# Converting double weights to float32 on chip: the exponent's offset moved from VectorE into ScalarE's scale

## The chip, the core and the metric

The kernel runs on one core of one Trainium2 chip. The metric is the device time of one execution in microseconds (us), lower is better. One core has a matrix engine (PE, TensorE), a vector engine (DVE, VectorE), a scalar engine (ACT, ScalarE), a general engine (POOL, GpSimd) and a sync engine (SP, SyncE) that issues most DMAs. Each engine works through its own instructions in order and waits on semaphores for the others.

## The reference

```python
x = attention(q, k, v, beta)          # a delta-rule recurrence over 768 steps, 32 heads of 48
x = x.transpose(...).reshape(3072, 384)
h = np.maximum(x @ w_in, 0.0)          # 384 x 2048
x = (h * h @ w_out).astype(np.float32)  # 2048 x 384
g = x @ w_gate                          # 384 x 1536
silu = g * (1.0 / (1.0 + np.exp(-g)))
return (silu * (x @ w_val) @ w_out2).astype(np.float32)
```

The five weight matrices arrive as float64, everything else as float32.

## The kernel before

There are three parts: the attention recurrence over six blocks J of 128 steps, a first pair of matrix products (w_in, relu squared, w_out), called moe1, and a second (w_gate, w_val, silu, w_out2), called moe2. For precision every operand of a large product is split into a high part rounded to PE's fp32r format and the rest, and three products are summed: high by high, high by rest, rest by high. PE's stream is written in program order; it computes moe1 of block J while the attention of block J + 1 is prepared, and moe2 at the end.

The weights come as 64-bit words, two int32 each, and are turned into float32 on chip, in pieces of 128x768 numbers. One `Piece` works as follows (line numbers of the kernel before):

- L171: ACT takes the absolute value of the upper word, read as a float, into the buffer `f` (there is one such buffer).
- L178: DVE takes the maximum of `f` and a constant. L180: DVE shifts `f` left by 3 bits and clears the top bits. L184: DVE puts in sign and the exponent's top bit from the upper word. L189: DVE adds the top three bits of the lower word. These are the piece's `STEPS`, four.
- `high` (L202): ACT copies the result into the weight tile, rounded. `low` (L205): the difference, on DVE in most of block 0, on POOL for the weights of moe2.

The 16 pieces of w_in and w_out (the last cut in two halves) are converted in the first 190 us, beside the end of the first attention block and moe1 of block 0; odd pieces are w_in, even ones w_out. `conv` is called with a number of pieces or half pieces while the attention starts up, and counts `int(STEPS * n)` steps; what is converted by then is `PRE`. From then on `conv_to` keeps the conversion a fixed number of steps ahead of the units of moe1. `conv_one` makes one step; it begins the next piece (its L171) behind the third operation, and behind the last operation it sends out the `low` of the piece before and this piece's `high`. The 18 pieces of moe2 are converted late in moe1, from 664 to 762 us, one `conv2_step` at a time.

A unit of moe1 is the following: PE makes h (L794, with x's high `xh` and rest `xl`), ACT relu (L797), square rounded to `hh` (L798) and square again (L802), DVE the rest `hl` (L804), then PE the second product `ps_y` (L820), whose last three groups read `hl`. In block 0 a unit is made for half the tokens (256 columns); later units have 512. The order of DVE, ACT and POOL in the overlapped parts is set by a scheduler at build time, with DVE, ACT and POOL in program order only in the startup and DVE later; so an edit of the pieces moves neighbours.

In moe2, ACT copies x rounded (`x2h`, L872), DVE makes the rest (`x2l`, L873).

Of the kernel before, what the change touches and what calls it, by code (L numbers as in the profile page):

```python
# [11 lines left out]
ACTF = mybir.ActivationFunctionType  # L12
ALU = mybir.AluOpType
AX = mybir.AxisListType


TINY = 2.0 ** -15


@with_exitstack  # L20
def delta_attention_moe_moe2_kernel(
# [35 lines left out]
    nc = tc.nc  # L57
# [12 lines left out]
    is64 = w_in.dtype == mybir.dt.int64  # L70
# [82 lines left out]
    class Piece:  # L153
# [2 lines left out]

        STEPS = 4 if is64 else 1

        def __init__(self, raw, place, blocks, lo):
            self.d = raw.rearrange("p (b f z) -> p z b f", b=blocks, z=Z)
            self.place, self.blocks, self.lo_eng = place, blocks, lo
            self.v = self.d[:, 1 if is64 else 0].bitcast(F32)
            self.left = self.STEPS
            if is64:

                n = self.d.shape[2] * self.d.shape[3]
                f = rp.tile([128, PIECE], F32, tag="f", bufs=1, name="f")[:, 0:n]
                self.f = f.rearrange("p (b f) -> p b f", b=blocks)  # L170
                nc.scalar.activation(out=self.f, in_=self.v, func=ACTF.Abs)  # L171
            self.steps = self.run()

        def run(self):
            if is64:
                f, fi = self.f, self.f.bitcast(I32)

                nc.vector.tensor_scalar(out=f, in0=f, scalar1=TINY, scalar2=None, op0=ALU.max)  # L178
                yield
                nc.vector.tensor_scalar(  # L180
                    out=fi, in0=fi, scalar1=3, scalar2=0x3FFFFFFF, op0=ALU.logical_shift_left, op1=ALU.bitwise_and
                )
                yield
                nc.vector.scalar_tensor_tensor(  # L184
                    out=self.d[:, 1], in0=self.d[:, 1], scalar=-0x40000000, in1=fi,
                    op0=ALU.bitwise_and, op1=ALU.bitwise_or,
                )
                yield
                nc.vector.scalar_tensor_tensor(  # L189
                    out=self.d[:, 1], in0=self.d[:, 0], scalar=29, in1=self.d[:, 1],  # L190
                    op0=ALU.logical_shift_right, op1=ALU.bitwise_or,
                )
            yield
# [23 lines left out]
    conv1 = [(pc, kd, 0) for pc in range(NP1) for kd in range(2)] + [(*LAST, 1)]  # L217
# [3 lines left out]
    making = []  # L221
    STEPS = Piece.STEPS

# [13 lines left out]
    def flush():  # L237
        while pending:
            pending.pop().low()
# [3 lines left out]
    def begin(job, lo):  # L243
        pc, kd, e = job
        if job in begun or job not in loaded:
            return
        raw = loaded.pop(job)

        def place():
            if e == 0:  # L250
                w1[pc, kd] = wp.tile([128, 2 * PIECE], F32R, tag="w", name="w1")
            return w1[pc, kd][:, e * PIECE:(e + 1) * PIECE] if job[:2] == LAST else w1[pc, kd]

        begun[job] = Piece(raw, place, 1 if job[:2] == LAST else 2 if kd else 2 * KD, lo)

    def conv_one(lo):

        if not making:
            job = conv1.pop(0)
            begin(job, lo)  # L260
            making.append(begun.pop(job))
        making[0].step()
        if making[0].left == STEPS - 3 and conv1:
            begin(conv1[0], lo)
        if making[0].left == 0:
            flush()
            making[0].high()
            pending.append(making.pop())

    def converted():  # L270

        return STEPS * (NCONV - len(conv1)) - sum(m.left for m in making)

    def conv_to(steps, lo):

        while converted() < min(steps, STEPS * NCONV) and (making or conv1[0] in loaded or conv1[0] in begun):
            conv_one(lo)

    def need(m, kd):

        i = 2 * (m // 2) + kd + (1 if (m // 2, kd) == LAST and m % 2 else 0)
        conv_to(STEPS * (i + 1), nc.vector)
        if converted() < STEPS * (i + 2):
# [640 lines left out]
    def run_all(names):  # L924
        for n in names:
            run(n)
# [31 lines left out]
    for b0 in (0, 64):  # L958
        nc.gpsimd.affine_select(
            out=mask[b0:b0 + 64], in_=mask[b0:b0 + 64], compare_op=ALU.is_ge, fill=1.0,  # L960
            base=0, pattern=[[-1, 64]], channel_multiplier=1,
        )
    for c in P2:
        k_load(1, c, nc.gpsimd)
    q_load(0, nc.gpsimd)
    run(("sq", 0, 0))
    run_all(("gram0", 0, 0, p) for p in P2)
    run(("root", 0, 0))
    run(("mb0", 0, 0, 0, nc.vector))
    run(("mb0", 0, 0, 1, nc.gpsimd))  # L970
# [238 lines left out]
```

## Time and profile before

| | |
|---|---|
| time, median of 3 runs | 1181.83 us (1181.17 to 1186.19) |
| profiled execution | 1185.92 us, its span 1184.1 us |
| mean granted TensorE clock | 0.946 of full speed |
| busy in the span: PE, DVE, ACT, POOL | 1087.6, 645.5, 385.2, 271.3 us |

Busy time is the time in which an engine executed instructions, so an engine that is 55% busy over the whole span can still be fully taken in a stretch of it. PE's time is 92% of the span; the question is what PE waits for in the other 8%, and where.

### The profile page before, as it was taken

What the parts mean: (1) busy time and instruction counts of PE and PEld (TensorE: products, weight loads), DVE (VectorE), ACT (ScalarE), POOL (GpSimd) and SP (SyncE); (2) the same over time, 40 slices, a digit from 0 to 9 for tenths busy, and PEclk for the clock granted to TensorE, in tenths of its full rate; (3) what the DMA queues carried; (4) which work ended last, traced back from release to release, by engine and by line L of the source; (5) the groups of instructions that cost most, each with busy time, mean ns of one, the idle gap of its engine ahead of it and who ended that gap; (6) DMA issues with size and microseconds to landing.
All of it is one profiled execution on the core that took longest, in us unless ns stands there. A gap on an engine that the chain in (4) does not pass through costs nothing. (4 is left out here: it accounts for less than half of the span.)

```text
span 1184.1 us, 25132 instructions
## 1 busy us (share of the span) xinstructions
PE 1087.6 (92%) x10863; PEld 905.3 (76%) x10863; DVE 645.5 (55%) x1116; ACT 385.2 (33%) x711; POOL 271.3 (23%) x394
## 2 busy tenths in 40 slices
PE   4378778999999999999999987899999999999998
PEld 4367667777888888788888865688888888888887
DVE  3859995456547546555543699834334343343333
ACT  1034563332233233323333666422122122122222
POOL 5067100480183166128000233300000000000000
PEclk8557887999999999999999999999999999999999
DMA  8537440461434326132211445301001010010000
GB/s 237 132 81 280 93 104 20 95 160 43 91 66 115 77 49 168 46 69 59 77 29 27 161 143 177 107 1 54 1 1 54 1 54 1 1 54 1 27 1 27
DMA packets 129119, 88.23 MB, mean 75 GB/s; under 512 B 103216, under 2 KB 107952, under 8 KB 129008
## 3 DMA queue, kind: packets, MB, share of 16 engines
q1 hardware_dynamic: 126656, 76.79, 24.6%
q0 software_dynamic: 2208, 9.57, 2.5%
q8 instruction: 85, 1.39, 0.5%
q10 hardware_dynamic: 144, 0.26, 0.1%
q14 instruction: 26, 0.21, 0.1%
HBM read 63.54 MB, written 23.07 MB: 73 GB/s over the span
## 5 line engine op out<-in xcount | busy, mean ns | idle before, releaser
L794 PE MATMUL ps_h<-xh,w 128*128 128x512 f32 (+1 forms) x684 | 215.3, 377 | 6.1 <-DVE w L205 5.5
L820 PE MATMUL ps_y<-hh,w 128*128 128x512 f32 (+1 forms) x654 | 158.5, 378 | 1.8 <-DVE w L205 1.7
L794 PEld LDWEIGHTS ps_h<-xh,w 128*128 128x128 f32 x684 | 129.9, 199 | 28.4 <-DVE w L205 6.1
L887 PE MATMUL ps_g<-x2h,w 128*128 128x512 f32 x432 | 145.9, 392 | 0.5 <-ACT x2h L872 0.5
L887 PE MATMUL ps_v<-x2h,w 128*128 128x512 f32 x432 | 144.9, 389 | 0.0
L797 ACT ACTIVATE r<-ps_h 128x512 f32<-128x512 f32 (+1 forms) x114 | 60.2, 528 | 248.0 <-PE ps_h L794 232.7
L891 DVE SCALAR_TENSOR_TENSOR th<-th,ps_g 128x512 f32<-128x512 f32 x72 | 49.4, 686 | 167.1 <-ACT th L890 166.9
L820 PEld LDWEIGHTS ps_y<-hh,w 128*128 128x128 f32 x654 | 113.4, 194 | 22.1 <-DVE w L205 2.2
L794 PE MATMUL ps_h<-xl,w 128*128 128x512 f32 (+1 forms) x342 | 126.7, 371 | 2.3 <-POOL xl L675 1.7
L800 DVE TENSOR_TENSOR r<-r 128x512 f32<-128x512 f32 (+1 forms) x72 | 50.3, 699 | 133.1 <-ACT hh L798 132.9
L912 PE MATMUL ps_o<-ph,w 128*128 128x512 f32 x432 | 111.9, 389 | 2.5 <-ACT ye L836 2.5
L820 PE MATMUL ps_y<-hl,w 128*128 128x512 f32 (+1 forms) x327 | 87.7, 378 | 18.9 <-DVE hl L804 18.9
L453 POOL TENSOR_TENSOR TMP<-T 128x30 f32<-128x30 f32 (+9 forms) x150 | 84.4, 563 | 82.5 <-DMA T<-m_scr 46.6
L890 ACT ACTIVATE th<-ps_g 128x512 f32<-128x512 f32 x72 | 43.0, 597 | 175.8 <-PE ps_g L887 175.8
L804 DVE TENSOR_TENSOR hl<-r,hh 128x512 fp32r<-128x512 f32 (+1 forms) x114 | 76.5, 671 | 43.0 <-ACT r L802 37.7
L912 PEld LDWEIGHTS ps_o<-ph,w 128*128 128x128 f32 x432 | 81.0, 188 | 19.6 <-ACT ye L836 2.9
L887 PEld LDWEIGHTS ps_g<-x2h,w 128*128 128x128 f32 x432 | 81.6, 189 | 17.9 <-ACT x2h L872 0.9
L460 POOL TENSOR_TENSOR T<-T,TMP 128x30 f32<-128x30 f32 (+9 forms) x150 | 91.9, 613 | 11.4
L887 PEld LDWEIGHTS ps_v<-x2h,w 128*128 128x128 f32 x432 | 81.2, 188 | 17.0
L894 ACT ACTIVATE ph<-th 128x512 fp32r<-128x512 f32 x72 | 45.5, 631 | 133.2 <-DVE th L892 133.2
L887 PE MATMUL ps_g<-x2l,w 128*128 128x512 f32 x216 | 84.7, 392 | 2.7 <-DVE x2l L873 2.7
L820 PEld LDWEIGHTS ps_y<-hl,w 128*128 128x128 f32 x327 | 58.9, 196 | 34.1 <-DVE hl L804 24.7
(128 smaller groups left out, 1839.3 us busy)
## 6 DMA issues: line engine op xcount, KB each, us to landing
raw<-in_moe_w_out_dram SPq DMA_DIRECT2D x12, 768.0 KB, 5.2
raw<-in_moe_w_in_dram SPq DMA_DIRECT2D x7, 768.0 KB, 9.0
m_scr<-M SPq DMA_DIRECT2D x20, 256.0 KB, 2.8
xs_scr<-ys SPq DMA_DIRECT2D x48, 96.0 KB, 2.2
xr<-xs_scr SPq DMA_DIRECT2D x12, 384.0 KB, 3.8
raw<-in_moe_w_gate_dram SPq DMA_DIRECT2D x6, 768.0 KB, 4.3
raw<-in_moe_w_val_dram SPq DMA_DIRECT2D x6, 768.0 KB, 4.4
x2raw<-y_scr SPq DMA_DIRECT2D x6, 768.0 KB, 4.6
```

What stands on the lines that cost most here:

```text
L453: eng.tensor_tensor(tmp[:, r0:r1], t_[:, r0:r1, kk:kk + 1].to_broadcast([n, r1 - r0, w]), t_[:, kk:kk + 1, kk + 1:].to_broadcast([n, r1 - ...
L460: eng.tensor_tensor(t_[:, r0:r1, kk + 1:], t_[:, r0:r1, kk + 1:], tmp[:, r0:r1], op=ALU.add)
L794: nc.tensor.matmul(ps, w_[:, kk], x_[:, kk, cols], start=n == 0, stop=n == 3 * KD - 1)
L797: nc.scalar.activation(out=r, in_=ps, func=ACTF.Relu)
L800: nc.vector.tensor_tensor(r, r, r, op=ALU.mult)
L804: eng.tensor_tensor(hl[:, at], r, hh[:, at].bitcast(F32), op=ALU.subtract)
L820: nc.tensor.matmul(acc[f], w_[:, fs], h_, start=first, stop=m == NM1 - 1 and n == 2)
L887: nc.tensor.matmul(ps, w_[:, kk], x_[:, kk], start=n == 0, stop=n == 3 * KD - 1)
L890: nc.scalar.activation(out=th, in_=gp, func=ACTF.Tanh, scale=0.5)
L891: nc.vector.scalar_tensor_tensor(out=th, in0=th, scalar=1.0, in1=gp, op0=ALU.add, op1=ALU.mult)
L894: nc.scalar.activation(out=hh, in_=th, func=ACTF.Copy)
L912: nc.tensor.matmul(o_acc[J][f], w_[:, fs], h_, start=m == 0 and n == 0, stop=m == NM2 - 1 and n == 2)
```

## The change

L171 gets a scale of 2^-112: ACT multiplies while it takes the absolute value, which takes the offset between the two formats' exponents off. The maximum (L178) goes, the shift (L180) needs no mask, and the mask of the next operation is the sign bit alone. `STEPS` is 3.

```diff
-TINY = 2.0 ** -15
+OFFSETS = 2.0 ** -112
...
-        STEPS = 4 if is64 else 1
+        STEPS = 3 if is64 else 1
...
-                nc.scalar.activation(out=self.f, in_=self.v, func=ACTF.Abs)
+                nc.scalar.activation(out=self.f, in_=self.v, func=ACTF.Abs, scale=OFFSETS)
...
-                nc.vector.tensor_scalar(out=f, in0=f, scalar1=TINY, scalar2=None, op0=ALU.max)
-                yield
-                nc.vector.tensor_scalar(
-                    out=fi, in0=fi, scalar1=3, scalar2=0x3FFFFFFF, op0=ALU.logical_shift_left, op1=ALU.bitwise_and
-                )
+                nc.vector.tensor_scalar(out=fi, in0=fi, scalar1=3, scalar2=None, op0=ALU.logical_shift_left)
                 yield
                 nc.vector.scalar_tensor_tensor(
-                    out=self.d[:, 1], in0=self.d[:, 1], scalar=-0x40000000, in1=fi,
+                    out=self.d[:, 1], in0=self.d[:, 1], scalar=-0x80000000, in1=fi,
...
-        if making[0].left == STEPS - 3 and conv1:
+        if making[0].left == STEPS - 2 and conv1:
             begin(conv1[0], lo)
```

In the changed kernel the shift is L178, the two following operations L180 and L185, `low` L201, `hl` L800. `conv(0.5)`, called six times beside one `conv(1)`, now makes `int(1.5)`, one step of three, where it made two of four: `PRE` is 9 steps, three pieces, where it was 16 steps, four pieces.

DVE in block 0 before, from the `low` of the third piece (a piece of w_in, whose weights h of units 2 and 3 reads) to the `hl` of unit 3; the `hl` between the two `low` rows is that of unit 1:

```order
L205 TENSOR_TENSOR w_1484<-raw,w_1484 128x6x128
L804 TENSOR_TENSOR hl<-r,hh 128x256
...
L205 TENSOR_TENSOR w_1531<-raw,w_1531 128x2x384
L804 TENSOR_TENSOR hl<-r,hh 128x256
...
L205 TENSOR_TENSOR w_1624<-raw,w_1624 128x6x128
L804 TENSOR_TENSOR hl<-r,hh 128x256
```

The same place in the changed kernel; the `hl` of units 0 and 1 stand in the first row of `hl`:

```order
L800 TENSOR_TENSOR hl<-r,hh 128x256 x2
L614 TENSOR_TENSOR RS_105<-ps_u,bB 64x384 x2
L178 TENSOR_SCALAR f<-f 128x768
L180 SCALAR_TENSOR_TENSOR raw<-raw,f 128x768
L185 SCALAR_TENSOR_TENSOR raw<-raw 128x768
L201 TENSOR_TENSOR w_1519<-raw,w_1519 128x6x128
L800 TENSOR_TENSOR hl<-r,hh 128x256
L614 TENSOR_TENSOR RS_106<-ps_u,bB 64x384 x2
L178 TENSOR_SCALAR f<-f 128x768
L180 SCALAR_TENSOR_TENSOR raw<-raw,f 128x768
L185 SCALAR_TENSOR_TENSOR raw<-raw 128x768
L201 TENSOR_TENSOR w_1611<-raw,w_1611 128x2x384
```

The third piece's `low` is w_1484 before and w_1519 now. Before, the `hl` of unit 2 stood behind the `low` of the fourth piece; now it stands right behind the `low` of the third.

DVE in the conversion for moe2, one piece and a unit of moe1 before:

```order
L178 TENSOR_SCALAR f<-f 128x768
L804 TENSOR_TENSOR hl<-r,hh 128x512
L180 TENSOR_SCALAR f<-f 128x768
L184 SCALAR_TENSOR_TENSOR raw<-raw,f 128x768
L189 SCALAR_TENSOR_TENSOR raw<-raw 128x768
```

And in the changed kernel:

```order
L178 TENSOR_SCALAR f<-f 128x768
L800 TENSOR_TENSOR hl<-r,hh 128x512
L180 SCALAR_TENSOR_TENSOR raw<-raw,f 128x768
L185 SCALAR_TENSOR_TENSOR raw<-raw 128x768
```

The shift now stands in the place of the maximum, ahead of `hl`, and the operation with sign and exponent follows `hl` directly. PE's order is the same in both kernels.

## Rows read from the trace of the kernel before

**Rows 1.** Windows: span, busy us of PE, PEld, DVE, ACT, POOL; PEclk, DMA, GB/s.
```profile
120.00:150.00 30.00, 21.00 (x181) 18.64 (x175) 27.49 (x38) 17.82 (x33) 5.54 (x4) 0.83 0.50 118
...
660.00:720.00 60.00, 53.51 (x227) 41.64 (x226) 55.26 (x56) 38.55 (x58) 20.54 (x10) 1.00 0.49 159
720.00:780.00 60.00, 51.32 (x213) 40.47 (x212) 49.31 (x57) 29.94 (x43) 18.14 (x12) 0.97 0.34 117
...
840.00:1184.00 344.00, 340.10 (x1501) 281.25 (x1499) 122.84 (x175) 78.16 (x124) 0.00 (x0) 1.00 0.05 19
```
**Rows 2.** PE's waits, 110 to 210 us: total us, times, longest.
```profile
PE ps_m L582 <- issue: 6.8, 1, 6.8
PE ps_y L820 <- DVE hl L804: 5.9, 4, 2.5
PE ps_h L794 <- DVE w L205: 5.5, 3, 3.0
```
**Rows 3.** PE's waits, 660 to 790 us.
```profile
PE ps_y L820 <- DVE hl L804: 8.2, 10, 0.9
PE ps_g L887 <- DVE x2l L873: 2.7, 1, 2.7
```
**Rows 4.** The maximum, all its instructions: shortest, median and longest in ns.
```profile
L178 DVE TENSOR_SCALAR f<-f x35: 351/560/1506, 63.8 to 754.7; 128x768 f32<-128x768 f32 x33, 128x384 f32<-128x384 f32 x2
```
**Rows 5.** Timeline of DVE, block 0: start, us, line, idle before.
```profile
151.71 0.55 DVE L178 TENSOR_SCALAR f<-f 128x768 f32<-128x768 f32 x1
152.29 0.56 DVE L180 TENSOR_SCALAR f<-f 128x768 int32<-128x768 int32 x1
152.89 0.96 DVE L184 SCALAR_TENSOR_TENSOR raw<-raw,f 128x768 int32<-128x768 int32 x1
```
**Rows 6.** Timeline of DVE as block 0 starts.
```profile
86.02 1.28 DVE L189 SCALAR_TENSOR_TENSOR raw<-raw 128x768 int32<-128x768 int32 x1
87.23 1.37 DVE L205 TENSOR_TENSOR w<-raw,w 128x768 fp32r<-128x768 f32 x1
...
91.60 1.41 DVE L675 TENSOR_TENSOR xl<-xr,xh 128x256 fp32r<-128x256 f32 x2 [1.84 <-ACT xh L673]
```
**Rows 7.** Timeline of DVE: a low of a w_in piece.
```profile
111.07 1.11 DVE L205 TENSOR_TENSOR w<-raw,w 128x768 fp32r<-128x768 f32 x1
```
**Rows 8.** Timeline of ACT: the unit that waits for that low.
```profile
113.37 0.38 ACT L797 ACTIVATE r<-ps_h 128x256 f32<-128x256 f32 x1 [0.98 <-PE ps_h L794]
...
114.23 0.42 ACT L802 ACTIVATE r<-r 128x256 f32<-128x256 f32 x1
```
**Rows 9.** Timeline of DVE: its longest idle times in block 0's conversion.
```profile
146.50 1.51 DVE L178 TENSOR_SCALAR f<-f 128x768 f32<-128x768 f32 x1 [1.83 <-ACT f L171]
...
177.13 0.42 DVE L804 TENSOR_TENSOR hl<-r,hh 128x256 fp32r<-128x256 f32 x1 [1.78 <-ACT r L802]
```
**Rows 10.** Timeline of DVE, one unit of the conversion for moe2.
```profile
682.59 0.96 DVE L189 SCALAR_TENSOR_TENSOR raw<-raw 128x768 int32<-128x768 int32 x1
683.54 0.56 DVE L178 TENSOR_SCALAR f<-f 128x768 f32<-128x768 f32 x1
684.05 0.69 DVE L804 TENSOR_TENSOR hl<-r,hh 128x512 fp32r<-128x512 f32 x1
...
685.31 2.48 DVE L184 SCALAR_TENSOR_TENSOR raw<-raw,f 128x768 int32<-128x768 int32 x1
687.82 0.96 DVE L189 SCALAR_TENSOR_TENSOR raw<-raw 128x768 int32<-128x768 int32 x1
```
**Rows 11.** Timeline of ACT, the same unit.
```profile
682.59 0.92 ACT L171 ACTIVATE f<-raw 128x768 f32<-128x768 f32 x1 [1.85 <-DVE raw L184]
...
683.92 0.89 ACT L202 ACTIVATE w<-raw 128x768 fp32r<-128x768 f32 x1
```
**Rows 12.** Timeline of POOL: the low of that unit, and a later one.
```profile
684.89 2.07 POOL L205 TENSOR_TENSOR w<-raw,w 128x768 fp32r<-128x768 f32 x1 [3.16 <-ACT w L202]
...
750.51 1.85 POOL L205 TENSOR_TENSOR w<-raw,w 128x768 fp32r<-128x768 f32 x1 [2.83 <-ACT w L202]
```

## The prediction

> **What bounds the kernel now.** I read the windows first, then PE's waits, then the timelines of the stretches in which PE waits. The windows divide the run into three kinds. From 840 us to the end PE is busy 340.10 of 344.00 us, and DVE 122.84: nothing taken off DVE there can be seen. In 120 to 150 us it is the other way round, DVE 27.49 of 30.00 and PE 21.00. In 660 to 720 us both are nearly full, DVE 55.26 and PE 53.51 of 60.00, and from 720 to 780 us PE has 51.32 [rows 1]. The two stretches in which PE has gaps are those in which weights are converted: block 0 up to 190 us (stage A), and 664 to 762 us (stage B). PE's waits name DVE in both. In A it waits 5.5 us for a `low`, 5.9 us for `hl`, and once 6.8 us ahead of `ps_m`, whose inputs DVE transposes [rows 2]. In B it waits 8.2 us for `hl` in ten waits and 2.7 us for `x2l` [rows 3]. After each stage PE is full again, so the time saved or lost in a stage is what moves the end.
>
> The change removes 35 maxima, 33 of them full, with a median of 0.560 us and 0.351 us for a half one [rows 4]. From start to start a full one costs 152.29 - 151.71 = 0.58 us of DVE [rows 5]. All 35 together are about 20 us of DVE; the question is how much of that PE gets.
>
> **Edits with one answer.** The shift with one operation and not two, and the sign mask, keep shape and type: I take 0.56 and 0.96 us as in [rows 5]. The scale on ACT's absolute value stays in the same pass, 0.92 us [rows 11]; if it cost something, 0.1 us would be covered in stage B, since `high` follows it only behind r and the second operation.
>
> **Stage A.** Thirteen full maxima and two halves stand on DVE between 95 and 173 us; 13 x 0.58 + 2 x 0.35 = 8.2 us go.
>
> Against that stands a side effect: `PRE` is three pieces and not four, so the conversion runs one piece less ahead of the units. This costs twice. First, L189 and `low` of the first piece ended at 88.6 us, in front of a wait of DVE for x (1.84 us idle, then `xl` at 91.60) that the change doesn't shorten [rows 6]. In the new order they stand behind the first block's AQ products, after 100 us: 88.60 - 86.02 = 2.6 us of work lose their cover. Second, `hl` of a unit now stands right behind the `low` that the unit itself (even units) or its second product (odd ones) needs, as the order shows, and DVE, in order, must wait there. How long: a `low` of a w_in piece ended at 111.07 + 1.11 = 112.18, the waiting unit's relu came at 113.37 and its second square ended at 114.23 + 0.42 = 114.65 [rows 7, 8]: 2.5 us from `low` to `hl`. Before, another piece's operations lay in that gap. I count hl2, hl4 and hl6 at 2.5 us each. For hl3 and hl5, whose h has its weights already, the bounds are 0 (h was done early) and 2.5; as the unit ahead was itself late I take 1.5 each. Sum 7.5 + 3.0 = 10.5 us. By unit 8 DVE is late and PE runs ahead, so I expect no such waits from there on.
>
> Part is given back, since DVE already lost time there that a later DVE would not lose again: 1.83 us idle before 146.50 and 1.51 - 0.56 = 0.95 us in that maximum, and 1.78 us idle before 177.13 [rows 9], together 4.6 us. The balance is 2.6 + 10.5 - 8.2 - 4.6 = +0.3 us. PE has then waited in five longer pieces; the granted clock is already 0.83 in such a stretch [rows 1], so part of its work is at the lower of its two levels. I estimate 0.5 us more for each wait (bounds 0, and 1.3 where half of a 2.5 us catch-up ran at half clock): 2.5 us. Stage A **loses about 3 us**. The bounds: with hl3, hl5 and hl6 not waiting and no clock lost, 2.6 + 5.0 - 8.2 - 1.8 = 2 us gained; with all five at 2.5, and only 1.83 given back, 2.6 + 12.5 - 8.2 - 1.8 + 2.5 = 7.6, about 8 us lost.
>
> **Stage B.** One unit runs from 682.59 to 687.82, 5.23 us [rows 10]. PE needs about 4.1 us for its 18 matmuls (18 x 340.10 / 1501, [rows 1]), so DVE's loop bounds. Take E = 682.56, the end of L184 before. L189 and ACT's next absolute value run side by side to E + 0.98; then come the maximum, `hl` (684.05, E + 1.49), the shift, and L184 at 685.31. But L184 takes 2.48 us there against 0.96 free [rows 5, 10]: POOL's `low` started at 684.89 and ended at 686.96 [rows 12], and L184 ends 0.83 us behind that. So the loop before is not DVE's sum: it is absolute value, r, `high` (683.92), POOL to 686.96, 0.83: the maximum is not in it. It is worth something only if its going lets L184 start ahead of POOL.
>
> By the rows it does. Without it the shift starts at E + 0.98, `hl` at 1.49, and L184 would come at 1.49 + 0.61 = 2.10; POOL comes at 684.89 = E + 2.33. L184 goes first and ends at 3.06. POOL follows with 1.85 us (the one that met no DVE at its start, [rows 12]) to 4.91, and now L189 is the one held, to 4.91 + 0.83 = 5.74. Then shift and `hl` take 1.12, L184 would be ready at 6.9; `high`, released by L189, brings POOL at 5.74 + 0.04 + 0.97 = 6.75, this time first. It ends at 8.7, L184 at 9.54. Two units take 9.54 in place of 10.46: 0.46 us per unit. Twelve units run in this rhythm, 5.5 us. The rest of the conversion, to 762 us, is mixed with moe2: `x2l` moves ahead of an `hl` and part of its 2.7 us of wait [rows 3] goes, while ACT's copies of moe1's last output come behind its next x copy and later; net I take 1 us. Stage B **gains about 6.5 us**. Bounds: 2 (nothing in the units, most of `x2l`), and 11 (all of 8.2 and 2.7, [rows 3]).
>
> This turn-taking is what the Trainium skill states in "SBUF — State Buffer", section "Who interferes with whom": a DVE instruction with two SBUF inputs and a GpSimd one exclude each other, and who issues first keeps the port for the whole instruction; the rows above agree (2.48 us against 0.96). By that rule alone, with POOL issuing first as it does in every unit now, the sum for B would be 2 us.
>
> **Sum.** 3 lost, 6.5 gained, 3.5 us less: the profiled execution's 1185.92 us would be 1182.4. That execution is 4.1 us above the median of the three runs, 1181.83; on it the forecast is 1178.3, rounded **1178 us**. A measurement here tells 0.5% from no change, 5.9 us, so 3.5 us would read as the same.
>
> **Rivals.**
> 1. *Slower: the lost piece of lead decides.* All five `hl` waits take the full 2.5 us, PE's clock drops further, and A loses 8; in B the start of L184 is no earlier and 2 is gained. 1181.8 + 6 = 1188 us. For it: DVE is full in A, so nothing covers a wait. Against: from unit 8 on each unit is 0.58 us shorter. It decides if hl8, which stood right ahead of the maximum at 151.71 [rows 5], comes more than 6 us later. Chance 0.20.
> 2. *POOL keeps the port.* The margin of L184 over POOL is 0.23 us (E + 2.10 against 2.33). If `hl` waits a little for r, POOL is first in every unit, the loop stays 5.23 and the maximum was hidden: B 2, A -3, 1183 us. Chance 0.20.
> 3. *No loss in A.* PE has h of the early units ready, the waits are short: A gains 2, B 7 to 8, 1172 us. Chance 0.14.
> 4. *Every maximum counts.* 33 x 0.56 less the covered first ones: 17 us, 1165 us. Against it are the idle times of DVE in A and the POOL loop in B. Chance 0.04.
> 5. *It does not do what it says.* The single shift, or the scaled absolute value, runs slower: at half the rate the shift costs 0.5 us more, just what was removed, A loses 8 and B gains 2 as in rival 1: 1188 us. Chance 0.04.
>
> The forecast itself has 0.38, from 1174 to 1184.
>
> **How the numbers follow.** Faster than 1175.9: rivals 3 and 4 (0.17) and nearly half of the forecast's spread (0.17), 0.34. Slower than 1187.7: rivals 1 and 5 mostly (0.18) and the tail of 2 (0.03), 0.21. The same: 0.45. The range leaves out rival 4 and the outer part of rival 3 below, and the outer part of rivals 1 and 5 above: 1169 to 1190 us.
>
> **What would show it.** Three operations per piece, 105 on DVE and not 140. In A: idle time of DVE before `hl`, released by ACT's r, in five units between 115 and 150 us; the shift behind hl8 some 5 us later than the maximum at 151.71, and hl14 (177.13 before, [rows 9]) 1 to 2 later. In B: units of 4.77 us, alternately one with L180 at 0.96 and L185 long and one the other way round; PE's wait for `hl` about 3 us and not 8.2. I am wrong if the units keep 5.23 us (rival 2), if DVE shows no idle time before hl2 to hl6 (rival 3), or if hl8 is over 6 us later (rival 1).

## The result: slower, and the profile after

The changed kernel takes 1192.37 us in the median of ten runs, the kernel before 1183.84 us in ten runs beside it: a ratio of 1.0068 with a 95% interval of 1.0039 to 1.0096, so 4.6 to 11.4 us slower. The forecast was 3.5 us less, 1178 us with a range of 1169 to 1190. The profiled execution of the changed kernel took 1191.95 us, its span is 1190.2 us.

DVE has less to do, and PE waits more. From part 1 of the profile's page after the change (busy us, share, instructions):

```profile
PE 1082.9 (91%) x10863; PEld 901.7 (76%) x10863; DVE 622.3 (52%) x1080; ACT 384.9 (32%) x711; POOL 269.8 (23%) x395
```

DVE lost 645.5 - 622.3 = 23.2 us of busy time, over the 20 us that were worked out for 35 maxima. The shift and the absolute value kept their price: their medians were 559 and 923 ns before. Their views now (count: shortest, median, longest ns):

```profile
L178 DVE TENSOR_SCALAR f<-f x35: 351/552/1551, 66.2 to 748.6; 128x768 int32<-128x768 int32 x33, 128x384 int32<-128x384 int32 x2
...
L172 ACT ACTIVATE f<-raw x35: 530/917/972, 65.3 to 745.9; 128x768 f32<-128x768 f32 x33, 128x384 f32<-128x384 f32 x2
```

The windows (columns as in [rows 1]):

```profile
120.00:150.00 30.00, 21.70 (x245) 19.67 (x245) 17.95 (x26) 14.52 (x28) 0.53 (x1) 0.78 0.18 40
...
720.00:780.00 60.00, 48.82 (x201) 38.64 (x200) 42.53 (x45) 27.72 (x40) 19.48 (x12) 0.94 0.33 113
```

Against [rows 1], DVE fell from 27.49 to 17.95 of 30 us in 120 to 150 us because it stood idle there (stage A below); PE fell from 51.32 to 48.82 in 720 to 780 us. PE's waits, first in 110 to 210 us, then in 640 to 790 us:

```profile
PE ps_h L790 <- DVE w L201: 12.2, 3, 4.4
PE ps_m L578 <- issue: 7.0, 1, 7.0
PE ps_y L816 <- DVE hl L800: 3.2, 3, 1.2
```
```profile
PE ps_y L816 <- DVE hl L800: 9.0, 9, 2.5
PE ps_o L908 <- ACT ye L832: 6.7, 1, 6.7
PE ps_y L816 <- ACT hh L794: 1.5, 1, 1.5
```

The wait for `ye` before, in 660 to 790 us:

```profile
PE ps_o L912 <- ACT ye L836: 2.5, 1, 2.5
```

PE's wait for a `low` rose from 5.5 us [rows 2] to 12.2. In the second stage the 2.7 us for `x2l` [rows 3] are gone, the 8.2 us for `hl` are 9.0, and a wait of 6.7 us for `ye`, the copy of moe1's last output out of PSUM, stands where 2.5 us were.

**Stage A.** DVE stands idle ahead of `hl`. The view of tile `hl` in 105 to 160 us, with what ended the idle time before it:

```profile
L800 DVE TENSOR_TENSOR hl<-r,hh x8: 416/425/427, 113.6 to 155.0; 128x256 fp32r<-128x256 f32 x8
its engine sat idle before it (us, times) until:
  ACT r L798: 13.2, 5
```

Five waits, 13.2 us. The first of them in the timeline of DVE:

```profile
118.15 0.95 DVE L201 TENSOR_TENSOR w<-raw,w 128x768 fp32r<-128x768 f32 x1
122.37 0.42 DVE L800 TENSOR_TENSOR hl<-r,hh 128x256 fp32r<-128x256 f32 x1 [3.27 <-ACT r L798]
```

The others are 1.27, 2.51, 2.14 and 4.04 us. The same view before has 11 `hl`, and DVE idle for 0.2 us:

```profile
L804 DVE TENSOR_TENSOR hl<-r,hh x11: 416/418/941, 109.5 to 159.9; 128x256 fp32r<-128x256 f32 x11
...
  ACT r L802: 0.2, 1
```

**Stage B.** Two units of the conversion for moe2, on DVE:

```profile
704.14 0.56 DVE L178 TENSOR_SCALAR f<-f 128x768 int32<-128x768 int32 x1
704.66 0.69 DVE L800 TENSOR_TENSOR hl<-r,hh 128x512 fp32r<-128x512 f32 x1
705.27 0.95 DVE L180 SCALAR_TENSOR_TENSOR raw<-raw,f 128x768 int32<-128x768 int32 x1
706.26 2.53 DVE L185 SCALAR_TENSOR_TENSOR raw<-raw 128x768 int32<-128x768 int32 x1
708.72 0.68 DVE L800 TENSOR_TENSOR hl<-r,hh 128x512 fp32r<-128x512 f32 x1
709.32 0.55 DVE L178 TENSOR_SCALAR f<-f 128x768 int32<-128x768 int32 x1
709.96 2.56 DVE L180 SCALAR_TENSOR_TENSOR raw<-raw,f 128x768 int32<-128x768 int32 x1
712.55 0.96 DVE L185 SCALAR_TENSOR_TENSOR raw<-raw 128x768 int32<-128x768 int32 x1
713.52 0.56 DVE L178 TENSOR_SCALAR f<-f 128x768 int32<-128x768 int32 x1
```

POOL's rests in the same two units:

```profile
705.49 2.48 POOL L201 TENSOR_TENSOR w<-raw,w 128x768 fp32r<-128x768 f32 x1 [3.15 <-ACT w L198]
709.83 1.88 POOL L201 TENSOR_TENSOR w<-raw,w 128x768 fp32r<-128x768 f32 x1 [1.85 <-ACT w L198]
```

This is the turn-taking of the forecast: in the first unit L180 comes ahead of POOL (0.95 us) and L185 is held (2.53), in the second L180 is held (2.56) and L185 free. Two units took 713.52 - 704.14 = 9.38 us; 9.54 was forecast, 10.46 they took before. The Trainium skill's "SBUF — State Buffer", section "Who interferes with whom", says that the engine which issues first keeps the shared port for its whole instruction; the trace agrees, with the holds of 2.53 and 2.56 us beside 0.95. But then ACT, with PE behind it:

```profile
748.12 0.90 ACT L198 ACTIVATE w<-raw 128x768 fp32r<-128x768 f32 x1 [1.36 <-DVE raw L185]
748.93 0.61 ACT L890 ACTIVATE ph<-th 128x512 fp32r<-128x512 f32 x1
749.45 1.47 ACT L868 ACTIVATE x2h<-x2raw 128x1536 fp32r<-128x1536 f32 x1
750.82 0.47 ACT L832 ACTIVATE ye<-ps_y 128x384 f32<-128x384 f32 x1
```
```profile
744.06 0.61 PE L908 MATMUL ps_o<-ph,w 128*128 128x512 f32 x2
751.34 2.08 PE L908 MATMUL ps_o<-ph,w 128*128 128x512 f32 x4 [6.66 <-ACT ye L832]
753.22 1.48 PE L908 MATMUL ps_o<-pl,w 128*128 128x512 f32 x3
```

The same copy and the same matmuls before:

```profile
745.56 0.47 ACT L836 ACTIVATE ye<-ps_y 128x384 f32<-128x384 f32 x1
```
```profile
746.09 1.21 PE L912 MATMUL ps_o<-ph,w 128*128 128x512 f32 x4 [2.45 <-ACT ye L836]
747.14 0.85 PE L912 MATMUL ps_o<-pl,w 128*128 128x512 f32 x3
```

The fourth and last copy of moe1's output ran at 750.82 behind the next block's x copy; before it ran at 745.56, ahead of it. The x copy is only 1.47 us of the delay: a piece's absolute value (745.86) and its `high` (748.12) stood ahead too, and `high` waited 1.36 us for an L185 that had itself taken 1.99 us on DVE beside a rest on POOL. PE, which needs that PSUM bank for `ps_o`, stood for 6.66 us, and its next matmuls ran slowly: the four and three above take 2.08 and 1.48 us where they took 1.21 and 0.85 before.

### The profile page after: what moved, and what is told of

It is laid out like the page before. It is cut to its first block, busy times and chain, and to the rows that moved or that the text cites. A ratio compares the mean times of both kernels' runs of the same rounds, so it can differ in the third digit from the quotient of the medians.

```text
span 1190.2 us, 25095 instructions
## 1 busy us (share of the span) xinstructions
PE 1082.9 (91%) x10863; PEld 901.7 (76%) x10863; DVE 622.3 (52%) x1080; ACT 384.9 (32%) x711; POOL 269.8 (23%) x395
## 5 line engine op out<-in xcount | busy, mean ns | idle before, releaser
L790 PE MATMUL ps_h<-xh,w 128*128 128x512 f32 (+1 forms) x684 | 214.1, 375 | 12.8 <-DVE w L201 12.8
L816 PEld LDWEIGHTS ps_y<-hh,w 128*128 128x128 f32 x654 | 113.3, 193 | 26.0 <-DVE w L201 4.1
L800 DVE TENSOR_TENSOR hl<-r,hh 128x512 fp32r<-128x512 f32 (+1 forms) x114 | 76.7, 673 | 52.9 <-ACT r L798 47.5
L456 POOL TENSOR_TENSOR T<-T,TMP 128x30 f32<-128x30 f32 (+9 forms) x150 | 88.8, 592 | 11.4
L883 PE MATMUL ps_v<-x2l,w 128*128 128x512 f32 x216 | 84.0, 389 | 0.0
```

What stands on the lines that cost most here:

```text
L456: eng.tensor_tensor(t_[:, r0:r1, kk + 1:], t_[:, r0:r1, kk + 1:], tmp[:, r0:r1], op=ALU.add)
L790: nc.tensor.matmul(ps, w_[:, kk], x_[:, kk, cols], start=n == 0, stop=n == 3 * KD - 1)
L800: eng.tensor_tensor(hl[:, at], r, hh[:, at].bitcast(F32), op=ALU.subtract)
L816: nc.tensor.matmul(acc[f], w_[:, fs], h_, start=first, stop=m == NM1 - 1 and n == 2)
L883: nc.tensor.matmul(ps, w_[:, kk], x_[:, kk], start=n == 0, stop=n == 3 * KD - 1)
```

## The experiments

Two theories were put against each other. **LEAD**: `PRE` fell from four pieces to three, and the conversion of block 0 now runs right in front of the units that need it; this is the loss. **END**: the loss is made at the end of moe1, where the last copy out of PSUM comes late. Later a third, **PORT**: in moe2's conversion DVE and POOL, taking turns, set the pace, whatever DVE's sum is.

All results in one table. "To A" is the start of the `hl` of the first unit with 512 columns (when block 0 is done), "middle" from there to the `hl` of the last unit ahead of moe2's conversion (660.16 before), where no experiment changes the program, and "B" from there to the first gate operation of the sixth unit of moe2 (770.76 before). These three come from one profiled execution each, in us; the ratio to the kernel before comes from five rounds of runs (for the changed kernel, the result above), its interval is the 95% one. Medians of different rows were not all taken side by side, so rows are best compared by their ratios.

| kernel | block 0's operations, lead | moe2's | to A | middle | B | median us | ratio (interval) |
|---|---|---|---|---|---|---|---|
| before | 4, four pieces | 4 | 198.1 | 462.1 | 110.6 | | 1 |
| the change | 3, three | 3 | 201.5 | 461.8 | 113.3 | 1192.37 | 1.0068 (1.0039 to 1.0096) |
| w2only | 4, four | 3 | 196.3 | 467.5 | 114.4 | 1187.44 | 1.0027 (1.0005 to 1.0048) |
| j0only | 3, three | 4 | 197.9 | 464.6 | 111.8 | 1190.47 | 1.0047 (1.0025 to 1.0068) |
| lead4 | 3, four | 3 | 185.7 | 462.1 | 113.3 | 1174.73 | 0.9915 (0.9884 to 0.9946) |
| before_lead3 | 4, three | 4 | 209.9 | 467.1 | 110.6 | 1200.31 | 1.0109 (1.0077 to 1.0141) |
| j0only_lead4 | 3, four | 4 | 185.4 | 461.0 | 110.8 | 1174.41 | 0.9904 (0.9877 to 0.9931) |
| oe4 | 3, three | 3, fourth buffer | 198.1 | 467.6 | 106.1 | 1184.82 | 1.0007 (0.9985 to 1.0029) |
| before_oe4 | 4, four | 4, fourth buffer | 197.2 | 461.4 | 108.7 | 1181.24 | 0.9968 (0.9947 to 0.9990) |
| lead4_oe4 | 3, four | 3, fourth buffer | 185.4 | 461.4 | 105.8 | 1167.89 | 0.9847 (0.9819 to 0.9874) |
| j0only_lead4_oe4 | 3, four | 4, fourth buffer | 182.8 | 462.4 | 108.6 | 1171.18 | 0.9887 (0.9865 to 0.9909) |
| lead5_oe4 | 3, five | 3, fourth buffer | 184.7 | 461.8 | 105.1 | 1167.40 | 0.9861 (0.9840 to 0.9881) |
| lead4_oe4_dvelow | 3, four | 3, buffer, low on DVE | 182.1 | 461.3 | 92.0 | 1155.11 | 0.9760 (0.9732 to 0.9788) |
| j0only_lead4_oe4_dvelow | 3, four | 4, buffer, low on DVE | 183.5 | 463.5 | 96.0 | 1159.15 | 0.9808 (0.9786 to 0.9830) |

**One half of the change at a time (w2only, j0only).** A piece gets its number of operations as an argument; everything else stays.

```diff
-        def __init__(self, raw, place, blocks, lo):
+        def __init__(self, raw, place, blocks, lo, ops=STEPS):
...
-                nc.scalar.activation(out=self.f, in_=self.v, func=ACTF.Abs, scale=OFFSETS)
+                nc.scalar.activation(out=self.f, in_=self.v, func=ACTF.Abs, scale=OFFSETS if ops == 3 else 1.0)
...
-        piece = Piece(raw2[pc, kind], lambda: t, 2 if kind == 2 else 2 * KD, nc.gpsimd)
+        piece = Piece(raw2[pc, kind], lambda: t, 2 if kind == 2 else 2 * KD, nc.gpsimd, 3)
```

> The change in the 18 pieces of moe2 alone; the first 16 pieces keep four operations and the lead of four pieces. Theory END (the time was lost at the end of the second conversion, where ACT's last copy of moe1's output now stands behind an x copy and PE waits 6.7 us for it): this kernel is slower than before by 3 to 6 us, with the 6.7 us wait of ps_o for ye and an offset of +2.5 to +3 us between the first moe1 unit of 512 columns and the fifth unit of moe2. Theory LEAD (the lost piece of lead in block 0 is the loss): no slower than before, 0 to 4 us faster. In both the first 200 us are those of before: hl behind its low of the next piece, no idle time over 2 us ahead of hl2 to hl6.

> The change in block 0's pieces alone, with its lead of three pieces; moe2's pieces keep four operations. Theory LEAD: 5 to 8 us slower than before, nearly the whole loss. Theory END: 1 to 3 us slower at most. In both the end of moe1 is that of before: a wait of about 2.5 us for ye, 2.7 us for x2l, and units of 5.2 us.

Measured: 1.0027 and 1.0047. Both halves lose, 0.6 to 5.7 us and 3.0 to 8.1 us, and together about what the whole change loses. w2only's PE waits 5.8 us for `ye`; j0only keeps the 2.5 us of before there, and shows 13.9 us of idle time ahead of `hl`. Neither theory alone is right.

**The lead put back (lead4).** The startup's steps are counted so that four pieces are converted:

```diff
-        conv_to(converted() + int(STEPS * n), lo)
+        conv_to(LEAD.pop(0), lo)
...
+    LEAD = [1, 3, 4, 6, 7, 10, 12]
```

> The changed kernel with the startup's steps counted so that four pieces are converted when the first unit starts (1, 3, 4, 6, 7, 10, 12 steps of 12 in place of 1, 2, 3, 4, 5, 8, 9). Theory LEAD: the idle times of DVE ahead of hl2 to hl6 go, and the kernel is as fast as before or up to 4 us faster: 5 to 10 us less than the changed kernel. Theory END: 2 to 3 us less than the changed kernel, still 3 to 6 us slower than before.

Measured: 0.9915, 6 to 14 us faster than before and, by the ratios, 18 less than the changed kernel, more than either theory said. Tile `hl` in 105 to 160 us:

```profile
L800 DVE TENSOR_TENSOR hl<-r,hh x12: 410/418/698, 108.1 to 157.5; 128x256 fp32r<-128x256 f32 x12
its engine sat idle before it (us, times) until:
  ACT r L798: 0.2, 1
```

The idle time is gone, twelve `hl` and not eight are done by 160 us, and block 0 ends 12.4 us sooner than before. Where the lead is kept, the maxima do come off the path.

**The lead taken from the kernel before (before_lead3).** Four operations everywhere, with `LEAD = [1, 2, 4, 5, 6, 10, 12]` of 16 steps.

> Four operations everywhere, as before, but the startup's steps counted so that three pieces and not four are converted when the first unit starts (1, 2, 4, 5, 6, 10, 12 of 16 steps): the lost lead alone, without the gain. Theory LEAD, with the sizes of the traces so far (13 us of idle time ahead of hl2 to hl6, 11.5 us gained in block 0 where the lead is kept): 9 to 15 us slower than before. Rival OPS (the schedule with three operations is itself what puts hl right behind its low, and the count of pieces matters little): 0 to 3 us slower.

Measured: 1.0109, 9 to 17 us slower, and the idle time is there with four operations too:

```profile
L808 DVE TENSOR_TENSOR hl<-r,hh x8: 424/426/1701, 112.7 to 158.6; 128x256 fp32r<-128x256 f32 x8
its engine sat idle before it (us, times) until:
  ACT r L806: 13.8, 6
```

This settles the lead: its loss makes the idle time by itself, and costs 12 to 14 us in block 0 (209.9 beside 196.3 to 198.1, one profile each).

**The lead kept, moe2's pieces as before (j0only_lead4).**

> Three operations in block 0's pieces with the lead of four pieces, four operations in moe2's. Theory LEAD plus END: 10 to 13 us faster than before, 2 to 3 us faster than the kernel with the lead kept and three operations everywhere. Rival: if the change in moe2's pieces is worth something by itself, 6 to 8 us faster than before only.

Measured: 0.9904 and 1174.41 us, beside 0.9915 and 1174.73 us with three operations in moe2 too. The first part of LEAD plus END holds, 8 to 15 us faster; of the further 2 to 3 us nothing can be told from runs that lie 0.3 us apart, though B is 2.5 us shorter in the profiles.

**A fourth output buffer (oe4, before_oe4, lead4_oe4, j0only_lead4_oe4).** The four copies of moe1's last block share three buffers, so the fourth waits for a transfer and is put behind other work of ACT. The edit, in both places that use these buffers:

```diff
-                    ye = pool2.tile([128, w], F32, tag="oe", bufs=3, name="ye")
+                    ye = pool2.tile([128, w], F32, tag="oe", bufs=4, name="ye")
```

> The changed kernel with four buffers and not three for the output copies of moe1's last block, so that the fourth copy need not wait for the first one's transfer: on ACT it then stands right behind the third, ahead of the x copy. Theory END: the 6.7 us wait of ps_o goes, with about 2 us of slow clock behind it, and the kernel gets back 5 to 8 us: -1 to +3 us against before. Theory LEAD: 0 to 3 us less than the changed kernel, still 5 to 8 us slower than before, since PE would then meet another wait there.

> The kernel before with four buffers for the output copies of moe1's last block and nothing else: what the buffer is worth without the change. Theory END: its wait for ye was 2.5 us, so 2 to 4 us faster than before. Rival BUFFER (the fourth buffer would give the same 7 us to any version, so it says nothing of the change): 6 to 8 us faster.

> The changed kernel with the lead of four pieces and with four buffers for the output copies of moe1's last block. Theory LEAD plus END: both losses go, 15 to 18 us faster than before, near 1167 us. Rival: the two hide each other, PE meeting another wait (hl, or x2l) at the end of moe1, 10 to 12 us faster only.

> Three operations in block 0's pieces with the lead of four, four operations in moe2's pieces, four buffers for the output copies: beside the same kernel with three operations in moe2's pieces too (1167.9 us, 1.5% under before) it gives what the change is worth in moe2's pieces once the copies don't wait. Theory END: the units' gain (4.9 us each and not 5.2) shows then, so this kernel is 2 to 5 us slower than that one, 1.1 to 1.3% under before. Rival: the gain in the units is taken back by x2l ahead of hl in any case, the two kernels are within 1.5 us.

Measured for oe4: 1.0007, by the ratios 7.2 us less than the changed kernel, as END said. PE's two largest waits in 640 to 790 us:

```profile
PE ps_y L816 <- DVE hl L800: 9.1, 9, 2.5
PE ps_y L816 <- ACT hh L794: 1.7, 1, 1.7
```

The wait for `ye` is gone, the others stayed. The same buffer is worth 1.2 to 6.3 us to the kernel before, whose wait was 2.5 us, and 1.9 us in B (110.6 to 108.7). The interval's end just touches the 6 to 8 us of rival BUFFER, but its middle, 3.8 us, and B speak against it: most of the wait is the change's. Both cures together give 0.9847, 15 to 21 us faster than before, as expected; neither takes the other's gain. And with the buffer, moe2's half of the change seems worth some 3 us: 1167.89 beside 1171.18 us, with intervals that still overlap, and B 105.8 beside 108.6.

**One more piece of lead (lead5_oe4).** `LEAD = [2, 4, 6, 7, 9, 13, 15]`.

> The changed kernel with five pieces converted when the first unit starts (2, 4, 6, 7, 9, 13, 15 steps) and four buffers for the output copies. Theory LEAD: four pieces are enough to keep another piece's operations between a low and its hl (0.2 us of idle time ahead of hl there); a fifth only puts its work in front of the first units: 0 to 4 us slower than with four. Rival: more lead is better still, 2 to 6 us faster than with four, near 1164 us.

Measured: 1167.40 us beside 1167.89, the same. Four pieces are enough.

**POOL out of the way (lead4_oe4_dvelow, j0only_lead4_oe4_dvelow).** The rests of moe2's weights are taken by DVE:

```diff
-        piece = Piece(raw2[pc, kind], lambda: t, 2 if kind == 2 else 2 * KD, nc.gpsimd)
+        piece = Piece(raw2[pc, kind], lambda: t, 2 if kind == 2 else 2 * KD, nc.vector)
```

> Lead of four, four buffers, and moe2's rests taken by DVE and not by POOL, so that the two don't exclude each other. If the turn-taking of DVE and POOL bounds the units (theory PORT): every operation of DVE has its free length (0.96 us), a unit takes 0.58 + 0.61 + 0.96 + 0.96 + 0.95, 4.1 us and not 4.9, and twelve of them give 6 to 9 us: 1159 to 1162 us. Rival: the transfers of the next pieces, or ACT, bound the units next, at 4.6 us or more: 0 to 4 us faster than with POOL.

> As the fastest kernel so far (lead of four, four buffers, moe2's rests on DVE), but with four operations in moe2's pieces: what the removed maximum is worth there once POOL no longer takes turns with DVE. Theory PORT: the unit of that kernel, some 3.9 to 4.0 us, is about PE's own 4.1 us; with the maximum back it is 4.5 to 4.6 us and PE waits for hl again, so this kernel is 6 to 10 us slower than 1155 us, 1161 to 1165 us. Rival: the units were bound by PE and had DVE time to spare, 0 to 2 us slower.

Measured: 1155.11 us, 0.9760. One unit on DVE:

```profile
674.46 0.68 DVE L800 TENSOR_TENSOR hl<-r,hh 128x512 fp32r<-128x512 f32 x1
675.22 0.56 DVE L178 TENSOR_SCALAR f<-f 128x768 int32<-128x768 int32 x1
675.82 0.96 DVE L180 SCALAR_TENSOR_TENSOR raw<-raw,f 128x768 int32<-128x768 int32 x1
676.69 0.95 DVE L201 TENSOR_TENSOR w<-raw,w 128x768 fp32r<-128x768 f32 x1
677.56 0.95 DVE L185 SCALAR_TENSOR_TENSOR raw<-raw 128x768 int32<-128x768 int32 x1
678.43 0.68 DVE L800 TENSOR_TENSOR hl<-r,hh 128x512 fp32r<-128x512 f32 x1
```

DVE does one operation more and the unit takes 3.97 us, and no operation is held. All that PE still waits for in 640 to 790 us:

```profile
PE ps_y L816 <- DVE hl L800: 1.1, 2, 0.6
```

PORT's forecast holds, by more than it said: 12.8 us less than with POOL by the medians, 10.3 by the ratios, 13.8 in B. The run takes two things away at once, the turns at the port and POOL's longer rest (1.88 us beside 0.95 on DVE); it does not part them. This is the fastest version, 2.1 to 2.7% under the kernel before. With four operations in moe2's pieces it is 1159.15 us: here the maximum costs 4.0 us by the medians and in B (96.0 beside 92.0), 5.7 by the ratios, under the 6 to 10 expected and over the rival's 2.

## Why the prediction was wrong

**The sum's stage B failed; stage A's total came out.** The forecast was 3 us lost in A and 6.5 gained in B; in B 2.7 were lost, 9.2 us away from it.

1. *A.* The lost lead was seen, and its mechanism is shown by lead4 and before_lead3. The five waits were put at 10.5 us and were 13.2: hl2 3.27, hl4 2.51 and hl6 4.04 for 2.5 each, hl3 1.27 and hl5 2.14 for 1.5 each. The three profiles with the changed block 0 reach the end of A at 201.5, 197.9 and 198.1 us, the three with the old one at 198.1, 196.3 and 197.2: about 2 us later (means 199.2 and 197.2). The signs that were named say the same: `hl8` came at 156.1 and 156.6 us in j0only and oe4 beside 151.4 before, some 5 us later as forecast, and `hl14` 1.4 and 1.9 us later. In the changed kernel's own profile `hl8` is 8.9 us later, which would be rival 1's sign, but there block 0's first `xl` already stood at 94.51 us beside 91.60 before, behind 5.77 us of idle time. The balance of +3 was about right as a small difference of two large sums, and in that it had luck: the maxima are worth 11 to 15 us there (lead4 and its kin reach A at 182 to 186 us), not 8.2, and the lost lead costs as much and 2 more. A part of what 8.2 left out is at `ps_m`: PE waits 5.0 and not 6.8 us there in lead4, and behind that wait the granted clock is 0.50 and then 0.99 (170 to 180 and 180 to 190 us), where before it was 0.50 and then 0.71 (180 to 190 and 190 to 200 us). As an estimate, that is 1.8 us of wait and 10 x (0.99 - 0.71) = 2.8 us of clock, 12.8 us with the 8.2.

2. *B, the units.* "Two units take 9.54 in place of 10.46" was right where the two engines met as described (9.38). Over the ten units from the `hl` at 674.52 to that at 723.41 a unit took (723.41 - 674.52) / 10 = 4.89 us and not 5.23, where 4.77 was forecast; in some units ACT's next absolute value waited for the weights' transfer. That is 3.4 us and not 5.5. (The forecast's own second rest, 8.7 - 6.75 = 1.95 us, is in no row; 1.88 was measured.) PE's wait for `hl` did not fall to 3 us either; it is 9.0. And the new order put two pieces between the `hl` at 667.89 and that at 674.52, 6.63 us in place of 3.66, which takes 3.0 of them back.

3. *B, the end.* This is the step that failed most: "ACT's copies of moe1's last output come behind its next x copy and later; net I take 1 us". The place was seen and priced far too low. The wait for `ye` went from 2.5 to 6.7 us, with slow matmuls behind it, and `x2l` ahead of an `hl` made PE wait 2.5 us there, while an `hh` stood 1.5 us behind an absolute value whose piece had not landed. In place of 1 us gained the end gave back the units' gain and more: over all of B 2.7 to 3.8 us lost in the three profiles with this half of the change and three buffers (113.3, 114.4, 113.3 beside 110.6 before). With a fourth buffer B goes to 106.1, which shows the `ye` wait as the larger part: where both kernels have that buffer the change gains 2.6 us in B (108.7 to 106.1), and without it loses 2.7. So of the 9.2 us, the late copy is 5.3, and the other 3.9 are the units' gain, forecast too large in item 2, and the `hl` and `hh` waits, which were not tried by themselves.

So the slower outcome came by another road than rival 1, which had A lose 8 us. Rival 2, POOL keeping the port, is wrong in six of the ten units (L180 is held in four), and right in that sharing the work with POOL sets the pace: without it the stretch falls to 92.0 us.

**What stays open.** The traces account for some 2 + 2.7 us, the lower end of the measured 4.6 to 11.4. By the changed kernel's own profile it is 3.4 - 0.3 + 2.7 = 5.8 of the 6.0 us between the two profiled executions, but 2.9 us of that are the late `xl`, which j0only and oe4, with the same block 0, do not show (88.79 and 89.91 us). Four profiles (w2only, oe4, j0only, before_lead3) spent 2.5 to 5.5 us more than the kernel before in the middle, in code that no version changes. In all four the granted clock is lower there: 0.91, 0.91, 0.93 and 0.91 in 235 to 310 us, beside 0.98 before and in the changed kernel. The windows of w2only and of the kernel before:

```profile
235.00:310.00 75.00, 69.88 (x875) 56.90 (x876) 39.68 (x78) 21.55 (x47) 28.60 (x47) 0.91 0.38 94
```
```profile
235.00:310.00 75.00, 69.55 (x930) 57.00 (x928) 42.94 (x82) 23.50 (x51) 30.18 (x49) 0.98 0.40 98
```

As an estimate, 75 x (0.98 - 0.91) = 5.3 us, about what w2only, oe4 and before_lead3 lost in the middle. It does not need a late block 0, since w2only has the old one; runs of one kernel lie up to 11 us apart (the kernel before: 1179.24 to 1190.54), and the profiled runs of w2only and before_lead3 are the slowest of theirs (1193.38 and 1202.85 us). Whether it comes more often behind a late block 0 was not settled.

## What to carry to other kernels

When an edit changes the number of steps of a pipelined piece, look at everything that counts in steps: here `int(STEPS * 0.5)` silently took a piece of lead away, worth as much in block 0 as the operation that was removed. Where two engines take turns at a port, add up the turns and not one engine's time: here DVE took the rest over from POOL, one more operation on the fuller engine, and the kernel got faster. A shorter loop also moves what a scheduler places behind it; the few instructions at a stage's end on which PE waits (here one copy out of PSUM) deserve a price of their own, and a buffer.

## What was not expected of the hardware

A `tensor_tensor` of 128x768 took DVE 0.95 us when it did moe2's rests itself; on POOL the same rest took 1.85 to 2.65 us, and a DVE operation beside it up to 2.66 us (0.95 free). Moving it was worth 10 to 13 us where the free lengths alone, 0.95 us more on DVE for each piece, said that DVE would be busier. And one stall of PE cost more than its length: behind the 6.66 us wait seven matmuls took 754.50 - 751.34 = 3.16 us, where before they took 747.83 - 746.09 = 1.74 us. The granted clock stood at 0.50, the lower of its two levels (1.2 GHz), in the 4.7 us behind the wait; behind the 2.5 us wait of before it stood at 1.00 (746.10 to 747.80 us), and the matmuls ran at their usual pace. Windows of the changed kernel:

```profile
751.30:754.50 3.20, 3.16 (x8) 2.48 (x9) 3.20 (x4) 0.93 (x1) 0.77 (x2) 0.50 0.17 61
754.50:756.00 1.50, 1.50 (x5) 1.21 (x4) 0.40 (x1) 0.00 (x0) 1.50 (x1) 0.50 0.00 0
```
